# Two gated linear-attention blocks on one core: order of the last G addition, source of the gate weights, and a split transpose copy

## The chip, the cores and the metric

The kernel runs on one core of one Trainium2 chip. The metric is device time in microseconds (us), as the median of three runs. A profile is one further execution, recorded by the hardware profiler; its span is counted from its first to its last recorded instruction.

## The reference

Two linear-attention blocks A and B read the same input x (2048 rows, 640 columns, bf16) with weights of their own, and a gate per row mixes their outputs:

```python
x = A_x                                                  # (1, 2048, 640)
g = sigmoid((x * gate_w).sum(-1, keepdims=True))         # gate_w: 640 numbers
def block(x, wqkv, wo):                                  # H = 32 heads of 20
    q, k, v = heads(x @ wqkv)
    pq, pk = phi(q), phi(k)                              # phi(t) = (t + 1 if t > 0 else exp(t)) + 1e-6
    kv = einsum("bhsd,bhse->bhde", pk, v); z = pk.sum(over s)
    o = einsum("bhqd,bhde->bhqe", pq, kv) / (einsum("bhqd,bhd->bhq", pq, z) + 1e-6)
    return merge_heads(o) @ wo
return g * block(x, A_wqkv, A_wo) + (1 - g) * block(x, B_wqkv, B_wo)
```

## The kernel before

Rows are cut into 16 chunks of 128 (`ST = 16`) and columns into 5 (`DT = 5`). Matrix products run on TensorE in bf16 and gather in PSUM; ScalarE does exp and copies out of PSUM; VectorE does the rest of phi, sums and products; GpSimd builds masks at the start; SyncE issues nearly all transfers. The value projection is never formed: phi(k)^T v is worked out as (x^T phi(k))^T Wv, so each block needs G = x^T phi(k) (the tile `GT`, 640x640).

The stages, in order:

1. `k_first`: the first four chunks of x are loaded in plain form and transposed on TensorE (`x_transpose`, L187). Its copy out of PSUM (L194) is cut at the columns named in `cuts`; chunks 0 and 1 use two copies, chunks 2 and 3 one. The other 12 chunks of x^T come by 15 transposing transfers from SyncE (L129).
2. A's k projection by chunks (`k_chunk`, matmuls L209, phi L199, L202, L206), with parts of A's q (`q_block`, `q_unit`) between, up to chunk 14. Then SyncE loads the plain rows of x for the rest (L647), A's value and output weights and B's key weights.
3. From here the order of the instructions is the written one (`tc.manual_schedule`). `gate_columns` (L159) turns `gate_w` from a row into 32 equal columns per part, `gwr`: the row `grow` was loaded by GpSimd (L126) at the start, five matmuls of one partition multiply it by ones (L163), and VectorE casts the result out of PSUM (L166). Then comes chunk 15, the rest of A's q, with the gate's logits (`gate_pass`, matmuls L173) and the sums of phi(k) (`z_rows`).
4. `g_all`: A's G. Part of it is plain (`g_pass`), the rest a 2x2 scheme with seven products (`g_strassen`, matmuls L314, additions L331). Between the products, `norm_unit` spreads the reciprocals of the denominators over the rows (matmuls L487), ScalarE copies them to bf16 (L500), and VectorE multiplies them into phi(q) (L501). This is done five times, two copies and two products each.
5. B's k projection, with A's `kvt_pass` and `m_unit` between; B's q; B's G by the same code as A's.
6. The end: `kvt_pass` for B (matmuls L401, masks L409) starts as soon as all of B's `GT` is there; `m_unit` multiplies by `wo`; then 8 pairs of output chunks (class `Pair`, matmuls L512, additions L517), with sums of phi(q) and of the M tiles (`p_sums`, `m_sums`, all at L451) between.

The end of `g_strassen` differs between the blocks. For A, the last norm unit follows the last addition into `GT`. For B it precedes the last product:

```python
        if b == 1:
            norm()
        g_prod(even, SX[4], b22, False)
        add(GT[:, 0:2, hi], even, u2)
        if b == 0:
            norm()
```

PSUM is handed out as four slots in rotation (`turn`). The first sum after B's G is `p_sums(part[0], (1,))`, on VectorE.

Of the kernel before, what the change touches and what calls it, by code (L numbers as in the profile page):

```python
# [8 lines left out]
P = 128  # L9
FP32 = mybir.dt.float32  # L10
BF16 = mybir.dt.bfloat16
ACT = mybir.ActivationFunctionType
ALU = mybir.AluOpType

S, D, H = 2048, 640, 32
Dh = D // H
DT = D // P
ST = S // P
# [3 lines left out]
HF = D // 2  # L22
# [3 lines left out]
RB = 256  # L26
# [4 lines left out]
def kernel(  # L31
# [11 lines left out]
    nc = tc.nc  # L43
# [4 lines left out]
    persist = ctx.enter_context(tc.tile_pool(name="persist", bufs=1))  # L48
    wpool = ctx.enter_context(tc.tile_pool(name="wpool", bufs=1))
    work = ctx.enter_context(tc.tile_pool(name="work", bufs=2))  # L50
# [3 lines left out]
    turn = [0]  # L54

    def ps_raw(name, slot=None):

        if slot is None:
            slot = turn[0]
            turn[0] = (slot + 1) % 4  # L60
        return psum.tile([P, 4 * HB], BF16, tag=f"ps{slot}", name=name)

    def ps(name, slot=None):

        return ps_raw(name, slot).bitcast(FP32).rearrange("p (b n) -> p b n", b=2)
# [5 lines left out]
    GT = persist.tile([P, DT, D], BF16, name="GT")  # L71
# [7 lines left out]
    ones = persist.tile([P, H], BF16, name="ones")  # L79
    gwr = persist.tile([P, DT, H], BF16, name="gwr")  # L80
    D3 = persist.tile([P, DT, SH], BF16, name="D3")
    hc, ic = ST // 2, 2 * P
# [39 lines left out]
    load_x(nc.scalar, 3, 4)  # L122
    wq[0] = wpool.tile([P, DT, D], BF16, tag="wq", name="wqA")
    nc.sync.dma_start(out=wq[0][:], in_=wq_dram[0][:, :, 0:D])
    grow = work.tile([1, D], BF16, tag="zr", name="grow")
    nc.gpsimd.dma_start(out=grow[:], in_=gate_w.rearrange("(o f) -> o f", o=1))  # L126
    for n in range(1, NB):
        for c in range(DT):
            nc.sync.dma_start_transpose(  # L129
                out=xT[:, c, n * HB:(n + 1) * HB], in_=x2[n * HB:(n + 1) * HB, c * P:(c + 1) * P]  # L130
# [8 lines left out]
    for sign, base in ((1, 0), (-1, Dh - 1)):  # L139
        nc.gpsimd.affine_select(  # L140
            out=maskE[:], in_=maskE[:], pattern=[[sign * P, DT], [-sign * Dh, H]],
# [3 lines left out]
    for r in range(4):  # L145
        rows = slice(32 * r, 32 * r + 32)
        for sign, base in ((1, 0), (-1, Dh - 1)):
            nc.gpsimd.affine_select(
                out=E4[rows], in_=E4[rows], pattern=[[sign, D]],
# [5 lines left out]
    one_l, one_r = [nc.const_aps.tensor(1.0, [P, n], BF16) for n in (P, HB)]  # L155
    for k in range(7):
        nc.tensor.matmul(warm[:, 0, :], lhsT=one_l, rhs=one_r, start=True, stop=True)

    def gate_columns():  # L159

        gps = ps("gps")
        for c in range(DT):
            nc.tensor.matmul(  # L163
                gps[:, 0, c * H:(c + 1) * H], lhsT=grow[0:1, c * P:(c + 1) * P], rhs=ones[0:1, :], start=True, stop=True
            )
        nc.vector.tensor_copy(out=gwr[:], in_=gps[:, 0, 0:DT * H].rearrange("p (c h) -> p c h", h=H))  # L166

    def by_group(dst, lhsT, src, h):

# [17 lines left out]
    def x_transpose(i, slot, eng, cuts=(0, DT)):  # L187
        pt = ps_raw("xt", slot)
        for c in range(DT):
            nc.tensor.transpose(out=pt[:, c * P:(c + 1) * P], in_=xn[:, i, c * P:(c + 1) * P], identity=ident[:])  # L190
        copy = nc.scalar.copy if eng == "act" else nc.vector.tensor_copy
        src = pt[:, 0:D].rearrange("p (c n) -> p c n", c=DT)
        for lo, hi in zip(cuts, cuts[1:]):
            copy(out=xT[:, lo:hi, i * P:(i + 1) * P], in_=src[:, lo:hi])  # L194
# [13 lines left out]
    def k_mm(b, i, c, pt, hf):  # L208
        nc.tensor.matmul(  # L209
            pt[:, hf, 0:HF], lhsT=xT[:, c, i * P:(i + 1) * P], rhs=wk[b][:, c, hf * HF:(hf + 1) * HF],  # L210
            start=(c == 0), stop=(c == DT - 1),
        )

    def k_done(b, i, pt):
        phi(pk[:, i, :].rearrange("p (b n) -> p b n", b=2), pt[:, :, 0:HF], HF)

    def k_chunk(b, i, slot=None):
        pt = ps(f"k{'AB'[b]}", slot)
        for hf in range(2):
            for c in range(DT):  # L220
                k_mm(b, i, c, pt, hf)
        k_done(b, i, pt)

    def k_first():

        pts = [ps("kA", (2 + i) % 4) for i in (0, 1)]

        def part(i, cs):
            for c in cs:
                for hf in range(2):  # L230
                    k_mm(0, i, c, pts[i], hf)

        for i in range(2):
            x_transpose(i, i, "dve", (0, 2, DT))
        for i in range(2):
            part(i, (0, 1))
        x_transpose(2, 0, "dve")
        for i in range(2):
            part(i, (2,))
        pts.append(ps("kA", 1))  # L240
        part(2, (0, 1, 2))
        x_transpose(3, 0, "dve")
        for i in range(3):
            part(i, (3, 4))
            k_done(0, i, pts[i])
        k_chunk(0, 3, 0)
# [55 lines left out]
    def k_sum(b, k):  # L302

        b11, b12 = [pk[:, 0:hc, n * HF:(n + 1) * HF] for n in range(2)]
        b21, b22 = [pk[:, hc:ST, n * HF:(n + 1) * HF] for n in range(2)]
        t = TK[b]
        left, right = {1: lambda: (b12, b11), 2: lambda: (b22, t[1]), 3: lambda: (b22, b12), 4: lambda: (b21, t[2])}[k]()
        add_rows(t[k], left, right, ALU.subtract)

    def g_prod(pt, left, right, first):  # L310

        for i in range(hc):
            for n in range(2):
                nc.tensor.matmul(  # L314
                    pt[:, n, 0:HF], lhsT=left[:, i, n * P:(n + 1) * P], rhs=right[:, i, :],
                    start=(first and i == 0), stop=(i == hc - 1), skip_group_check=not first,
                )

    def g_strassen(b, norm):

        x11, x12 = [xn[:, k:k + hc, 0:ic] for k in (0, hc)]
        x22 = xn[:, hc:ST, ic:2 * ic]
        b11 = pk[:, 0:hc, 0:HF]
        b21, b22 = [pk[:, hc:ST, n * HF:(n + 1) * HF] for n in range(2)]
        lo, hi = slice(0, HF), slice(HF, D)

        def temp(name):
            return work.tile([P, 2, HF], FP32, tag="osb", name=name, bufs=3)

        def add(dst, pt, sb):  # L330
            nc.vector.tensor_tensor(out=dst, in0=pt[:, :, 0:HF], in1=sb[:], op=ALU.add)  # L331

        even, odd = ps("gs0", 0), ps("gs1", 1)
        g_prod(even, x11, b11, True)
        p1 = temp("p1")
        nc.scalar.copy(out=p1[:], in_=even[:, :, 0:HF])
        g_prod(odd, SX[2], TK[b][2], True)
        u2 = temp("u2")
        add(u2[:], odd, p1)
        k_sum(b, 4)  # L340
        norm()
        g_prod(even, x12, b21, False)
        nc.scalar.copy(out=GT[:, 0:2, lo], in_=even[:, :, 0:HF])
        norm()
        if b == 0:
            x_sum(4)
        g_prod(odd, SX[3], TK[b][3], False)
        u3 = temp("u3")
        add(u3[:], odd, p1)
        norm()  # L350
        even = ps("gs0", 0)
        g_prod(even, SX[1], TK[b][1], True)
        add(GT[:, 2:4, hi], even, u3)
        norm()
        g_prod(odd, x22, TK[b][4], False)
        add(GT[:, 2:4, lo], odd, p1)
        if b == 1:
            norm()
        g_prod(even, SX[4], b22, False)
        add(GT[:, 0:2, hi], even, u2)  # L360
        if b == 0:
            norm()

    def z_rows(b):

# [116 lines left out]
    def norm_unit(b, parts, rts, slots):  # L482

        pts = [ps(f"ex{'AB'[b]}", s) for s in slots]
        for k, (m, h) in enumerate(parts):
            for j in range(4):
                nc.tensor.matmul(  # L487
                    pts[j // 2][:, j % 2, k * RB:(k + 1) * RB], lhsT=E4[32 * j:32 * j + 32, m * P:(m + 1) * P],
                    rhs=rts[h][32 * j:32 * j + 32, :], start=True, stop=True,
                )  # L490
        (m0, h0), (m1, h1) = parts
        for jj in range(2):
            src = pts[jj][:].rearrange("p j (k n) -> p j k n", n=RB)
            if h0 == h1:
                r0 = h0 * 2 * HB + jj * HB
                dst = pqT[b][:, m0:m1 + 1, r0:r0 + HB].rearrange("p k (j n) -> p j k n", n=RB)
            else:
                dst = pqT[b][:, m0, :].rearrange("p (k u j n) -> p u j k n", k=2, u=2, n=RB)[:, jj]
            ex = work.tile([P, 2, 2, RB], BF16, tag="ex", name="ex")
            nc.scalar.copy(out=ex[:], in_=src)  # L500
            nc.vector.tensor_tensor(out=dst, in0=ex[:], in1=dst, op=ALU.mult)  # L501

    def rows_of(i):
# [131 lines left out]
    with tc.manual_schedule():  # L635
        k_first()
# [4 lines left out]
        for m in (0, 2):  # L641
            q_block(0, m, n)
    q_unit(0, DT - 1, 0)
    for i in range(hc, ST - 1):
        k_chunk(0, i)
    for n in range(1, NB):
        nc.sync.dma_start(  # L647
            out=xn[:, n * CB:(n + 1) * CB, :], in_=x2[n * HB:(n + 1) * HB, :].rearrange("(q p) d -> p q d", p=P)
        )
# [8 lines left out]
        return pool.tile([P, HB] if n == 1 else [P, n, HB], FP32, tag=name, name=name)  # L658

    with tc.manual_schedule():  # L660
        gate_columns()
        k_chunk(0, ST - 1)
        k_sum(0, 1)
        zsel = q_pass(0, [(m, 1) for m in range(DT)])
# [41 lines left out]
        with late_pool("single") as single:  # L706
            halves = [[bank(single, f"s{c}{hf}") for hf in range(2)] for c in (3, 4)]
            for c in (3, 4):
                pts = [t[:, 0:HF] for t in halves[c - 3]]
# [19 lines left out]
        for i in range(1, half):  # L729
            p, after = pairs[i], pairs[i + 1] if i + 1 < half else None  # L730
# [53 lines left out]
```

## Time and profile before

| what | before |
|---|---|
| median of 3 runs | 196.92 us (196.78 to 197.01) |
| profiled execution, its time | 196.04 us |
| its span | 194.3 us |
| granted TensorE clock, mean | 0.996 of full |
| TensorE busy | 97% of the span |
| VectorE busy | 80% |
| ScalarE busy | 44% |
| DMA queue 1 (SyncE) | 17694 packets, 13.34 MB, 25.2% of 16 engines' span |

A line of the timeline or of the chain begins with the start in us from the span's start and the duration in us. In the timeline follow engine (PE is TensorE, DVE VectorE, ACT ScalarE, POOL GpSimd, SPq SyncE's queue), line, operation, output and inputs with shapes, and the count, where neighbouring instructions are merged. A bracket gives how long the engine sat idle before, and what released it. Matmuls overlap, so their modelled ends may pass the start of the next. The chain of work that ended last is followed back from the last instruction; "issue" is time in which the engine waited for nothing that the profile shows.

### The profile page before, as it was taken

Reading aid. Unit: us, or ns where it says so; the run is one execution under the profiler, and the core shown is the slowest. Engines: PE = TensorE matmul, PEld = TensorE weight load, DVE = VectorE, ACT = ScalarE, POOL = GpSimd, SP = SyncE. Lnnn points to the kernel's source line nnn. Section 1 sums busy time; section 2 is a strip of 40 time slices with the busy share of each in tenths; the row PEclk is TensorE's granted clock in tenths of the full one; section 3 lists DMA queues with packets and bytes.
Section 4 is the critical chain, followed back from the end, with each engine's and each line's share of the span. In section 5 each row is a group of like instructions: output and inputs, shape, how many; then the busy total and the mean of one; then the engine's idle time right before and its main releaser. Section 6 shows DMA issues by size and latency. Waiting matters only on the chain.

```text
span 194.3 us, 3665 instructions
## 1 busy us (share of the span) xinstructions
PE 188.6 (97%) x1497; PEld 120.8 (62%) x1504; DVE 155.4 (80%) x258; ACT 84.9 (44%) x111; POOL 9.2 (5%) x23
## 2 busy tenths in 40 slices
PE   8999999999999999999999999999998999999992
PEld 3556557664576666877764444576667776777771
DVE  4388869888989796888786689999787899888553
ACT  2055455455931874356562455413874611111110
POOL 7920000000000000000000000000000000000000
PEclk9999999999999999999999999999999999999998
DMA  6975469960050000220062000000000001322112
GB/s 188 312 159 77 97 186 371 240 191 3 2 169 3 0 0 3 72 97 3 0 140 55 2 0 0 0 3 0 0 3 0 0 3 67 126 78 71 67 67 71
DMA packets 18318, 14.22 MB, mean 73 GB/s; under 512 B 8782, under 2 KB 18302, under 8 KB 18302
## 3 DMA queue, kind: packets, MB, share of 16 engines
q1 hardware_dynamic: 17694, 13.34, 25.2%
q10 hardware_dynamic: 576, 0.66, 1.0%
q8 instruction: 12, 0.20, 0.4%
q14 instruction: 4, 0.03, 0.1%
q0 software_dynamic: 32, 0.00, 0.0%
HBM read 9.40 MB, written 2.62 MB: 62 GB/s over the span
## 4 chain that ended last, share of the span: by engine, by line
PE 91%; DMA 2%; DVE 2%; issue 1%; ACT 1%; ACTq 0%; DVEq 0%
PE gs L314 15%; PE kB L209 11%; PE qB L254 11%; PE kA L209 11%; PE qA L254 7%; PE ox L512 5%; PE oy L512 5%; PE oz L512 5%; PE qA L265 4%; DMA xn<-in_A_x_dram 2%; PE ow L512 2%; PE gB L287 2%; PE gA L287 2%; PE mA L427 1%; DVE osb L517 1%; PE exB L487 1%
## 5 line engine op out<-in xcount | busy, mean ns | idle before, releaser
L209 PEld LDWEIGHTS <-xT 128*128 128x128 bf16 x320 | 30.8, 98 | 12.8 <-DVE xT L194 0.4
L202 DVE TENSOR_SCALAR e<-e 128x640 bf16<-128x640 bf16 (+1 forms) x52 | 18.8, 361 | 9.3 <-ACT e L199 8.3
L209 PE MATMUL kA<-wkA,xT 128*128 128x320 bf16 x160 | 23.0, 299 | 0.0
L209 PE MATMUL kB<-wkB,xT 128*128 128x320 bf16 x160 | 22.9, 299 | 0.0
L254 PE MATMUL qB<-xT,wqB 128*128 128x512 bf16 x97 | 21.9, 379 | 0.2
L199 ACT ACTIVATE e<-kA 128x640 bf16<-128x640 f32 x16 | 11.1, 704 | 13.6 <-PE kA L209 13.6
L254 PEld LDWEIGHTS <-wqB 128*128 128x128 bf16 x100 | 9.6, 98 | 11.4 <-issue 0.3
L199 ACT ACTIVATE e<-kB 128x640 bf16<-128x640 f32 x16 | 11.3, 705 | 10.7 <-PE kB L209 10.7
L199 ACT ACTIVATE e<-qB 128x1024 bf16<-128x1024 f32 x10 | 10.2, 1024 | 13.1 <-PE qB L254 10.7
L199 ACT ACTIVATE e<-qA 128x1024 bf16<-128x1024 f32 x10 | 10.2, 1024 | 10.5 <-PE qA L265 5.2
L206 DVE SCALAR_TENSOR_TENSOR pk<-kB,e 128x640 bf16<-128x640 f32 x16 | 13.2, 824 | 1.7
L206 DVE SCALAR_TENSOR_TENSOR pk<-kA,e 128x640 bf16<-128x640 f32 x16 | 13.2, 824 | 1.6
L254 PE MATMUL qA<-xT,wqA 128*128 128x512 bf16 x58 | 13.5, 379 | 0.1
L206 DVE SCALAR_TENSOR_TENSOR pqTB<-qB,e 128x1024 bf16<-128x1024 f32 x10 | 12.2, 1224 | 1.0
L549 ACT COPY u<-ox 128x320 f32<-128x320 f32 x8 | 3.4, 426 | 20.9 <-PE ox L512 20.9
L500 ACT CAST ex<-exA 128x1024 bf16<-128x1024 f32 x10 | 9.6, 1017 | 5.8 <-PE exA L487 4.9
L314 PEld LDWEIGHTS <-xn 128*128 128x128 bf16 x96 | 8.9, 98 | 4.5 <-issue 1.3
L314 PEld LDWEIGHTS <-S 128*128 128x128 bf16 x96 | 9.1, 98 | 4.2 <-issue 0.8
L500 ACT CAST ex<-exB 128x1024 bf16<-128x1024 f32 x10 | 9.6, 1017 | 3.7 <-PE exB L487 3.7
L512 PEld LDWEIGHTS <-xT 128*128 128x128 bf16 x85 | 8.0, 98 | 3.0 <-DVE xT L451 0.2
L254 PEld LDWEIGHTS <-wqA 128*128 128x128 bf16 x60 | 5.7, 97 | 6.7 <-issue 0.3
L512 PEld LDWEIGHTS <-pqTA 128*128 128x128 bf16 x85 | 8.0, 98 | 2.9
(118 smaller groups left out, 301.7 us busy)
## 6 DMA issues: line engine op xcount, KB each, us to landing
out_dram<-osb SPq DMA_DIRECT2D x15, 160.0 KB, 1.8
xn<-in_A_x_dram SPq DMA_DIRECT2D x3, 640.0 KB, 5.7
wqA<-in_A_wqkv_dram SPq DMA_DIRECT2D x1, 800.0 KB, 6.0
wvA<-in_A_wqkv_dram SPq DMA_DIRECT2D x1, 800.0 KB, 9.3
wkB<-in_B_wqkv_dram SPq DMA_DIRECT2D x1, 800.0 KB, 4.6
wqB<-in_B_wqkv_dram SPq DMA_DIRECT2D x1, 800.0 KB, 4.5
wvB<-in_B_wqkv_dram SPq DMA_DIRECT2D x1, 800.0 KB, 4.5
woA<-in_A_wo_dram SPq DMA_DIRECT2D x1, 750.0 KB, 12.0
```

Of the source, the lines that this page charges most:

```text
L199: nc.scalar.activation(out=e[:], in_=src, func=ACT.Exp)
L202: nc.vector.tensor_scalar(e[:], e[:], 1.0, EPS, op0=ALU.min, op1=ALU.add)
L206: nc.vector.scalar_tensor_tensor(out=dst, in0=src, scalar=1.0 + EPS, in1=e[:], op0=ALU.add, op1=ALU.max)
L209: nc.tensor.matmul(pt[:, hf, 0:HF], lhsT=xT[:, c, i * P:(i + 1) * P], rhs=wk[b][:, c, hf * HF:(hf + 1) * HF], start=(c == 0), stop=(c == D ...
L254: nc.tensor.matmul(pt[:, u, :], lhsT=wq[b][:, c, m * P:(m + 1) * P], rhs=xT[:, c, n * HB:(n + 1) * HB], start=(c == 0), stop=(c == DT - 1),)
L265: nc.tensor.matmul(pt[:, u, :], lhsT=wq[b][:, c, (m + u) * P:(m + u + 1) * P], rhs=xT[:, c, n * HB:(n + 1) * HB], start=(c == 0), stop=(c ...
L287: nc.tensor.matmul(pt[:, hf, 0:HF], lhsT=xn[:, i, c * P:(c + 1) * P], rhs=pk[:, i, hf * HF:(hf + 1) * HF], start=(i == 0), stop=(i == ST - 1),
L314: nc.tensor.matmul(pt[:, n, 0:HF], lhsT=left[:, i, n * P:(n + 1) * P], rhs=right[:, i, :], start=(first and i == 0), stop=(i == hc - 1), s ...
L427: nc.tensor.matmul(dst, lhsT=KVT[:rows, j, c * P:(c + 1) * P], rhs=wo_sb[b][:rows, j, hf * HF:(hf + 1) * HF], start=(k == 0), stop=(k == 1),)
L500: nc.scalar.copy(out=ex[:], in_=src)
L512: nc.tensor.matmul(dst, lhsT=left[:, c, r0:r0 + P], rhs=right[:, c, :], start=(first and c == 0), stop=(c == DT - 1), skip_group_check=not ...
L549: nc.scalar.copy(out=self.u2[:], in_=self.at("x"))
```

## The change

There are three edits.

- In `g_strassen`, the last addition into `GT[:, 0:2, hi]` becomes two, one per 128-row block. `norm_unit` no longer multiplies; it returns its two pending products, and a new function `scale` issues them. For every norm unit but B's last this leaves the order as it was. For B's last, the first product stays ahead of the last addition and the second goes behind it.
- `gate_columns`, its five matmuls and its cast are gone. `gate_w` is loaded as a tile `gcol` of 128 partitions by 5, one element at a time, by SyncE after the 15 transposes and before the plain rows of x. One VectorE copy spreads it over the 32 columns of `gwr`; it stands between the phi of chunk 14 and the phi of chunk 15. The slot that the gate's matmuls had is skipped.
- The copy of chunk 2's transposed x is cut in two, after 2 of 5 column parts, as for chunks 0 and 1.

```diff
-    grow = work.tile([1, D], BF16, tag="zr", name="grow")
-    nc.gpsimd.dma_start(out=grow[:], in_=gate_w.rearrange("(o f) -> o f", o=1))
+    gcol = persist.tile([P, DT], BF16, name="gcol")
...
-    def gate_columns():
-
-        gps = ps("gps")
-        for c in range(DT):
-            nc.tensor.matmul(
-                gps[:, 0, c * H:(c + 1) * H], lhsT=grow[0:1, c * P:(c + 1) * P], rhs=ones[0:1, :], start=True, stop=True
-            )
-        nc.vector.tensor_copy(out=gwr[:], in_=gps[:, 0, 0:DT * H].rearrange("p (c h) -> p c h", h=H))
...
-        x_transpose(2, 0, "dve")
+        x_transpose(2, 0, "dve", (0, 2, DT))
...
-        norm()
+        scale(norm())
...
         add(GT[:, 2:4, lo], odd, p1)
-        if b == 1:
-            norm()
+        late = norm() if b == 1 else []
+        scale(late[0:1])
         g_prod(even, SX[4], b22, False)
-        add(GT[:, 0:2, hi], even, u2)
-        if b == 0:
-            norm()
+        for n in range(2):
+            nc.vector.tensor_tensor(out=GT[:, n, hi], in0=even[:, n, 0:HF], in1=u2[:, n], op=ALU.add)
+        scale(late[1:] if b == 1 else norm())
...
+        muls = []
         for jj in range(2):
...
             ex = work.tile([P, 2, 2, RB], BF16, tag="ex", name="ex")
-            nc.scalar.copy(out=ex[:], in_=src)
+            nc.scalar.copy(out=ex[:], in_=pts[jj][:].rearrange("p j (k n) -> p j k n", n=RB))
+            muls.append((dst, ex))
+        return muls
+
+    def scale(muls):
+        for dst, ex in muls:
             nc.vector.tensor_tensor(out=dst, in0=ex[:], in1=dst, op=ALU.mult)
...
-    for i in range(hc, ST - 1):
+    for i in range(hc, ST - 2):
         k_chunk(0, i)
+    with nc.allow_non_contiguous_dma(reason="640 elements, one to a partition and column"):
+        nc.sync.dma_start(out=gcol[:], in_=gate_w.rearrange("(c p) -> p c", p=P))
...
     with tc.manual_schedule():
-        gate_columns()
+        k_chunk(0, ST - 2)
+        turn[0] = (turn[0] + 1) % 4
+        nc.vector.tensor_copy(out=gwr[:], in_=gcol[:, :, None].to_broadcast([P, DT, H]))
         k_chunk(0, ST - 1)
```

More of the change, by code (lines that the diff above doesn't have):

```diff
@@ L340, in g_strassen @@
         k_sum(b, 4)
-        norm()
+        scale(norm())
         g_prod(even, x12, b21, False)
         nc.scalar.copy(out=GT[:, 0:2, lo], in_=even[:, :, 0:HF])
-        norm()
+        scale(norm())
         if b == 0:
@@ L349, in g_strassen @@
         add(u3[:], odd, p1)
-        norm()
+        scale(norm())
         even = ps("gs0", 0)
@@ L353, in g_strassen @@
         add(GT[:, 2:4, hi], even, u3)
-        norm()
+        scale(norm())
         g_prod(odd, x22, TK[b][4], False)
         add(GT[:, 2:4, lo], odd, p1)
-        if b == 1:
-            norm()
+        late = norm() if b == 1 else []
+        scale(late[0:1])
         g_prod(even, SX[4], b22, False)
-        add(GT[:, 0:2, hi], even, u2)
-        if b == 0:
-            norm()
+        for n in range(2):
+            nc.vector.tensor_tensor(out=GT[:, n, hi], in0=even[:, n, 0:HF], in1=u2[:, n], op=ALU.add)
+        scale(late[1:] if b == 1 else norm())
     def z_rows(b):
@@ L491, in norm_unit @@
         (m0, h0), (m1, h1) = parts
+        muls = []
         for jj in range(2):
-            src = pts[jj][:].rearrange("p j (k n) -> p j k n", n=RB)
             if h0 == h1:
```

## The prediction

> **What bounds the kernel now.** I read the page first (busy shares, the chain by engine), then the chain in order of time to find the places where it leaves TensorE, then the timeline around each edit, and the SyncE queue last because one transfer is moved onto it. The built order of both kernels gave the order on each engine and which earlier instruction each one waits for.
>
> From the page, part 1 and the first line of part 4:
>
> ```profile
> PE 188.6 (97%) x1497; PEld 120.8 (62%) x1504; DVE 155.4 (80%) x258; ACT 84.9 (44%) x111; POOL 9.2 (5%) x23
> PE 91%; DMA 2%; DVE 2%; issue 1%; ACT 1%; ACTq 0%; DVEq 0%
> ```
>
> TensorE is busy 97% of the span and carries 91% of the chain. So an edit pays in two ways only: by taking matmuls away from TensorE, or by closing one of the few gaps in the chain. The chain in order of time (start, us, who) shows the three places that the diff touches:
>
> ```profile
> 7.04 0.54 PE kA L209 x4
> 7.58 0.04 issue
> 7.63 0.99 PE kA L209 x6
> ...
> 28.11 9.51 PE kA L209 x70
> 37.62 0.22 PE gps L163 x5
> 37.83 1.47 PE kA L209 x10
> 39.30 0.21 PE qA L254
> ...
> 147.49 0.69 DVE pqTB L501
> 148.18 0.74 DVE GT L331
> 148.92 0.04 issue
> 148.96 1.59 PE mid L401 x30
> ```
>
> The first is a tiny break, where chunk 2's transposed x is copied out. The second is the gate's five matmuls. The third is the one long stretch in the middle of the kernel in which the chain runs over VectorE: a normalisation product (L501), then the last addition of x^T phi(k) (L331), and only then B's kvt matmuls. The timeline there:
>
> ```profile
> 145.43 2.35 PE L314 MATMUL gs<-pk,MB 128*128 128x320 bf16 x16
> 147.49 0.69 DVE L501 TENSOR_TENSOR pqTB<-ex,pqTB 128x1024 bf16<-128x1024 bf16 x1 [0.22 <-ACT ex L500]
> 147.61 0.84 PE L512 MATMUL ox<-MA,pqTA 128*128 128x320 bf16 x5
> 148.10 0.81 DVE L331 TENSOR_TENSOR GT<-gs,u 128x640 bf16<-128x640 f32 x1
> 148.83 0.81 DVE L451 TENSOR_TENSOR pqTA<-pqTA,pqTB 128x1280 bf16<-128x1280 bf16 x1
> 148.96 1.59 PE L401 MATMUL mid<-GT,wvB 128*128 128x120 bf16 x30 [0.51 <-DVE GT L331]
> ```
>
> The addition's last input, the gs product, is ready at 145.43 + 2.35 = 147.78, but VectorE starts the addition at 148.10: a product that nothing waits for yet stands ahead of it. TensorE idles 0.51 us.
>
> **The change, part by part.**
>
> *B's last addition.* On TensorE and ScalarE the order is as before. On VectorE the last normalisation product goes behind the addition, and the addition becomes two of 128x320. By the built order the first waits for the last gs matmul of both blocks, the second for nothing more, and kvt's first matmul waits for the second. So there is no early start from the row blocks; the gain is the product moved out of the way. VectorE started a sum 0.04 us after its product's end at A's counterpart (75.33 after 70.84 + 4.45 = 75.29). So the first half starts at 147.82. Nearest row for its cost: osb<-oz, 128x320 out of PSUM, 490 ns, with the next one starting 0.41 later (159.07, 159.48). The second half runs from 148.23 to 148.72, and with the 0.05 that kvt took after the old addition (148.91 to 148.96) it starts at 148.77: **0.19 us** earlier. A single addition at 147.82 would end at 147.82 + 0.81 = 148.63, so the halving itself gives back 0.09. Bounds: the gain can't pass the idle 0.51; if the first half starts 0.10 late (as the u sum at 134.77 did behind two waits) and the halves do not overlap, kvt starts at 147.88 + 0.98 + 0.05 = 148.91 and the gain is 0.05. I take 0.19, since the pairs of L517 do overlap.
>
> What is queued behind: the product (starts 148.23 + 0.40 = 148.63; pairs of L501 lie 0.6 apart), then p_sums' addition at 149.23, which frees VectorE 0.73 later, at 149.96. The KVT masks need it when kvt's matmuls end, 148.77 + 1.59 = 150.36. That is 0.40 us of cover, where it was 0.95. Without it, the masks and then B's m_unit would come late by what is missing. ScalarE needs no buffer from the product before 157. In A the halved addition costs VectorE about 0.08 us at 75.33, and kvtA comes at 78.45: nothing.
>
> *The gate.* Five matmuls of one row each and their weight loads leave TensorE. From the end of chunk 14 to the first q matmul it took 39.30 - 37.62 = 1.68 us. A chunk without company takes 9.51 / 7 = 1.36. So **0.32 us** goes: the 0.22 of the matmuls and 0.10 of slower start of chunk 15. Low bound 0.22, high bound 0.40 (the weight loads' idle of 0.26 before them included in part). Chunk 15's PSUM slot is that of chunk 12, whose phi ended at 36.92, so it doesn't wait.
>
> VectorE's cast of gwr (314 ns) is replaced by a spread copy out of SBUF, moved one chunk later: behind chunk 14's phi, ahead of chunk 15's. The trace has no copy with a repeated input; I bound it by 0 and the 0.31 of the old cast, and take 0.31 (same 160 outputs). Chunk 14's phi frees VectorE at about 39.55, so gwr is there at about 39.9. The logit matmuls that read it start at 41.46 - 0.32 = 41.14: cover 1.2 us. Chunk 15's exp ends at 40.04 - 0.32 = 39.72, so its phi loses at most 0.15, and z's matmuls that read it come two us later: nothing.
>
> *The transfer* moves from GpSimd's queue to SyncE's, as 640 elements, between the transposes and x's rows:
>
> ```profile
> 4.34 20.95 SPq L129 DMA_TRANSPOSE xT<-in_A_x_dram  x15
> 25.33 1.68 SPq L647 DMA_DIRECT2D xn<-in_A_x_dram  x3
> 27.06 0.91 SPq L586 DMA_DIRECT2D wvA<-in_A_wqkv_dram  x1
> 28.01 0.97 SPq L591 DMA_DIRECT2D woA<-in_A_wo_dram  x1
> ```
>
> All transposes stay ahead of it. An issue costs 0.37 to 0.97 there. No row has a transfer of single elements. Bounds of its landing: 3.6 us (the old transfer of the same 1.2 KB) and 12.4 us (woA's last piece, the longest of all), so between 29 and 38 us, against 39.55 when VectorE wants it. Queue q1's packets took 25.2% of 16 x 194.3 us over 17694, or 44 ns each; 640 of them over 16 engines, spread evenly (an estimate), are 1.8 us, so I take the early end. It puts x's rows (5.7 us to landing) at some 33 to 36 us; their first reader is x_sum at 45.71. wvA, woA and wkB are wanted after 75. Nothing on the path. GpSimd loses a 0.61 us issue at 1.29; its identity was ready 1 us before the first transpose anyway.
>
> A rule speaks against this edit. The Trainium skill, "DMA: Bandwidth & Descriptors", section "Rules for kernel authors", says that a strided last dimension becomes one descriptor per element and should be made contiguous; its "Specifications" add that pieces under 512 B cost a read-modify-write. No run here shows such a transfer yet. By the rule it is slow, but only the second rival below would let that reach the time.
>
> *Chunk 2's copy in two* (292 and 348 ns in the rows of chunks 0 and 1, against 492): the first half is there at 7.08 + 0.29 = 7.37, before 7.58, and the second, wanted 4 matmuls later at 8.12, by about 7.7. The break of **0.04** closes. If the fourth chunk of x or wk's last piece lands just in time behind it, 0.
>
> Sum: 0.32 + 0.19 + 0.04 = **0.55 us**. The profiled execution took 196.04 with its span of 194.3 and would take 195.5; it lies 0.88 under the median of 196.92. The difference carries over, since later waits all hang on TensorE (ScalarE's exps wait for matmuls, VectorE for ScalarE): 196.4. About 0.2% (0.39 us) is what a measurement of this kernel can tell from no change.
>
> **The rivals.**
>
> 1. *It shrinks below what can be told.* Only the matmuls' own 0.22 goes (the 0.10 stays as a change-over elsewhere), the tail gives its low bound of 0.05, and the copy nothing: 0.27 us, 196.65. For it: the two steps of 0.10 rest on modelled ends. Against: chunks before it show 1.36 each without exception. Chance 0.23.
>
> 2. *Slower: the gate's column lands late.* VectorE then stands at the spread copy, with chunk 15's phi and k_sum behind it, and TensorE waits at the logits. It decides from a landing after 40.8 (41.14 less the copy): 15 us after issue at 25.4, or 360 ns per element on 16 engines, eight times the 44 ns. Were the elements served by only one engine, 640 x 44 ns = 28 us: landing near 54, 13 us late, 210 us. For it: no row of such a transfer. Against: even woA, queued behind five others, took 12.4. Chance 0.07.
>
> 3. *Row blocks do not pay:* the halves delay kvt and the product behind them pushes p_sums over the masks. VectorE would have to lose 0.40 more than counted; then kvt gains 0.19 and the masks lose it again: 0.36 in all, 196.56, within what can't be told. Chance 0.05.
>
> **How the numbers follow.** The forecast has 0.65 and gives "faster", its own range being a gain of 0.39 to 0.95 (0.40 + 0.51 + 0.04), 195.97 to 196.53. Rivals 1 and 3 are "same", 0.23 + 0.05. Rival 2, 0.07, is "slower"; nothing else here reaches that side. The range goes from 196.0, the high bounds, to 197.0, rival 1 with the spread of the runs above the median (0.09); it leaves out rival 2 and the edges.
>
> **What would show it.** In the changed profile: no gps; from the end of chunk 14 to the first q matmul 1.36 instead of 1.68; kvtB's mid 0.19 sooner after the last gs product, with VectorE's two 128x320 additions directly behind it and the last L501 product after them; masks waiting for mid and not for p_sums; no wait at 7.6; gcol landing before 38. A VectorE wait for a DMA near 39.5, masks behind p_sums, or a new TensorE gap at 43 or 57 would make it wrong.

## The result, and the profile after

| what | before | after |
|---|---|---|
| median of 10 runs each, on one chip | 196.89 us (196.18 to 197.44) | 195.69 us (194.78 to 196.60) |
| ratio | | 0.9936, interval 0.9913 to 0.9959 |
| profiled execution: time, span | 196.04, 194.3 us | 195.64, 193.8 us |

The change made the kernel faster by 1.26 us (0.81 to 1.71 by the interval). 0.55 was forecast, so the direction was right and the size was less than half of what came; 195.69 lies below the range. Two more timings of the same source gave 0.9937 each, and one of the kernel before 0.9993, so this is no accident of one run.

The page after, part 1, the first line of part 4, and two lines of part 3 (queue: packets, MB, share):

```profile
PE 189.2 (98%) x1499; PEld 121.2 (63%) x1499; DVE 155.6 (80%) x261; ACT 84.9 (44%) x111; POOL 8.5 (4%) x22
...
q1 hardware_dynamic: 18350, 13.34, 25.2%
...
q8 instruction: 11, 0.18, 0.4%
...
PE 96%; DVE 2%; ACT 0%; issue 0%; DVEq 0%; ACTq 0%
```

The step from 91% to 96% is no gain of that size. In this execution the chain runs back to the start over the warm-up matmuls, and in the one before over the landing of x's third chunk; which of the two comes last varies between executions of either kernel. Two smaller lines will matter below: q1 has 656 packets more (18350 for 17694), and q8 fetched 11 blocks of instructions where it was 12.

The chain of waits after, at the three places of the change:

```profile
7.08 0.28 PE xt L180 x5
7.36 1.38 PE kA L199 x10
...
9.01 2.99 PE kA L199 x22
...
28.22 10.87 PE kA L199 x80
39.09 2.16 PE qA L244 x10
...
145.29 2.29 PE gs L304 x16
147.59 0.02 issue
147.61 0.90 DVE GT L351 x2
148.51 0.04 issue
148.55 1.59 PE mid L391 x30
```

The ten matmuls behind chunk 2's transposes are one piece of 1.38; before they were 0.54, a break of 0.04, and 0.99. The weight loads of the last six of them, which need the copy, show what was closed (first before, then after; the bracket is the wait for the copy):

```profile
7.62 0.66 PEld L209 LDWEIGHTS <-xT 128*128 128x128 bf16 x6 [0.37 <-DVE xT L194]
```

```profile
7.74 0.66 PEld L199 LDWEIGHTS <-xT 128*128 128x128 bf16 x6 [0.17 <-DVE xT L184]
```

The gate's matmuls are gone from between chunks 14 and 15: 80 matmuls in 10.87, which is eight times 1.36. The last gs product is followed by the additions after 0.02 us, and there is no normalisation product in the chain any more. Note also that chunk 2's transposes start at 6.91 in the timeline here and at 6.59 in the profiled execution of before: this pair of spans (0.5 apart) hides some 0.3 us of the gain, since the execution after came to them later.

The timeline after B's last G product:

```profile
147.61 0.89 DVE L351 TENSOR_TENSOR GT<-gs,u 128x320 bf16<-128x320 f32 x2 [0.55 <-PE gs L304]
...
148.41 0.68 DVE L496 TENSOR_TENSOR pqTB<-ex,pqTB 128x1024 bf16<-128x1024 bf16 x1
148.55 1.59 PE L391 MATMUL mid<-GT,wvB 128*128 128x120 bf16 x30 [0.30 <-DVE GT L351]
...
150.18 0.66 DVE L399 TENSOR_TENSOR KVT<-mid,maskE 120x120 bf16<-120x120 f32 x3 [0.35 <-PE mid L391]
```

VectorE waits 0.55 for the product instead of being late for it, the product of phi(q) runs behind the additions, and the masks still wait for TensorE, with 0.35 us of cover left (0.40 was forecast).

SyncE's queue after, and VectorE's copy that replaces the cast:

```profile
4.36 21.02 SPq L128 DMA_TRANSPOSE xT<-in_A_x_dram  x15
25.42 0.58 SPq L642 DMA_DIRECT2D gcol<-in_gate_w_dram  x1
26.05 1.62 SPq L644 DMA_DIRECT2D xn<-in_A_x_dram  x3
```

```profile
39.68 0.31 DVE L660 COPY gwr<-gcol 128x160 bf16<-128x160 bf16 x1
```

The gate's column is issued at 25.42 in 0.58 us, lands 4.2 us after the start of its issue, and is read ten microseconds after that.

### The profile page after: what moved, and what is told of

The parts are those of the page before. It is cut to its first block, busy times and chain, and to the rows that moved or that the text cites. A ratio compares the mean times of both kernels' runs of the same rounds, so it can differ in the third digit from the quotient of the medians.

```text
span 193.8 us, 3662 instructions
## 1 busy us (share of the span) xinstructions
PE 189.2 (98%) x1499; PEld 121.2 (63%) x1499; DVE 155.6 (80%) x261; ACT 84.9 (44%) x111; POOL 8.5 (4%) x22
## 3 DMA queue, kind: packets, MB, share of 16 engines
q1 hardware_dynamic: 18350, 13.34, 25.2%
## 4 chain that ended last, share of the span: by engine, by line
PE 96%; DVE 2%; ACT 0%; issue 0%; DVEq 0%; ACTq 0%
PE gs L304 16%; PE kA L199 12%; PE kB L199 11%; PE qB L244 11%; PE qA L244 7%; PE ox L507 5%; PE oy L507 5%; PE oz L507 5%; PE qA L255 4%; PE ow L507 2%; PE gA L277 2%; PE gB L277 2%; PE warm L156 2%; PE mA L417 1%; DVE osb L512 1%; PE exA L477 1%
## 5 line engine op out<-in xcount | busy, mean ns | idle before, releaser
L199 PE MATMUL kA<-wkA,xT 128*128 128x320 bf16 x160 | 23.5, 307 | 0.0
L189 ACT ACTIVATE e<-qB 128x1024 bf16<-128x1024 f32 x10 | 10.2, 1024 | 13.1 <-PE qB L244 13.1
L189 ACT ACTIVATE e<-qA 128x1024 bf16<-128x1024 f32 x10 | 10.2, 1024 | 10.5 <-PE qA L255 5.2
## 6 DMA issues: line engine op xcount, KB each, us to landing
wvA<-in_A_wqkv_dram SPq DMA_DIRECT2D x1, 800.0 KB, 10.2
```

What stands on the lines that cost most here:

```text
L189: nc.scalar.activation(out=e[:], in_=src, func=ACT.Exp)
L199: nc.tensor.matmul(pt[:, hf, 0:HF], lhsT=xT[:, c, i * P:(i + 1) * P], rhs=wk[b][:, c, hf * HF:(hf + 1) * HF], start=(c == 0), stop=(c == D ...
```

## The experiments

After the result some 0.7 us (1.26 less 0.55) had no place. The runs below tell apart: terms that were mis-sized; a cost that GpSimd's early transfer had in the kernel before; a start that merely varies; and, at the end, an instruction fetch. All ratios are against the kernel before, run in turn on the same chip; 0.001 is 0.20 us.

| run | ratio | interval |
|---|---|---|
| e1 before, row loaded by SyncE late | 0.9996 | 0.9975 to 1.0017 |
| e2 after, with GpSimd's row load added | 0.9956 | 0.9935 to 0.9978 |
| e3 end of B's G alone | 0.9980 | 0.9961 to 0.9999 |
| e4 gate alone | 0.9972 | 0.9950 to 0.9993 |
| e5 cut copy alone | 0.9999 | 0.9980 to 1.0017 |
| e6, e10 after again | 0.9937, 0.9937 | 0.9912 to 0.9961, 0.9917 to 0.9956 |
| e7 before, ten warm-ups more | 1.0078 | 1.0053 to 1.0104 |
| e8 after, ten warm-ups more | 1.0037 | 1.0015 to 1.0058 |
| e9 before again | 0.9993 | 0.9969 to 1.0017 |
| e11 after, copy whole | 0.9957 | 0.9932 to 0.9983 |
| e12 after, addition whole | 0.9939 | 0.9916 to 0.9962 |
| e17 before, twenty TensorE instructions more | 0.9986 | 0.9967 to 1.0005 |
| e18 after, ten TensorE instructions more | 0.9961 | 0.9938 to 0.9984 |

**e1 and e2: the transfer on GpSimd.** The gate's five matmuls stay in e1, and only the row's load moves; e2 gives the kernel after an unused load of the row on GpSimd.

```diff
 e1, in before.py
-    nc.gpsimd.dma_start(out=grow[:], in_=gate_w.rearrange("(o f) -> o f", o=1))
+    ... the same by nc.sync, ahead of the plain rows of x
 e2, in after.py
+    grow = work.tile([1, D], BF16, tag="zr", name="grow")
+    nc.gpsimd.dma_start(out=grow[:], in_=gate_w.rearrange("(o f) -> o f", o=1))
```

> The kernel before with one edit: the row of gate weights is loaded by SyncE, after the transposes, and no longer by GpSimd at the start; the five matmuls stay. The change gave 1.2 us where its three steps add up to 0.55. Theory S: the other 0.65 is a cost of GpSimd's transfer at the start, which the profiled execution of before doesn't show; then this gives 0.65 us, a ratio of about 0.9967. Theory N: the steps give 0.55 and the rest is the spread of the executions; then this is 1.000. Theory T: the rest lies in the tail or at the gate's matmuls; then this is 1.000 too.

> The changed kernel with GpSimd's transfer of the row put back at the start; nothing reads the row. Theory S: only the three steps are left, 0.55 us, a ratio of about 0.9972, against 0.9936 for the change. Theories N and T: as the change itself, 0.9972 by N (its true size), 0.994 by T.

e1 does not move the time by anything that can be told, and its interval leaves out the 0.9967 of theory S: GpSimd's transfer does not cost 0.65 us, and that theory falls. The interval of e2 holds the forecasts of all three. Both traces come back below, where the end of the span shows a small cost that neither ratio resolves.

**e3, e4, e5: each part alone, and e6 after once more.**

```diff
 e3: before.py with g_strassen and norm_unit of after.py
 e4: before.py with gcol, its transfer and the gwr copy of after.py
 e5, in before.py
-        x_transpose(2, 0, "dve")
+        x_transpose(2, 0, "dve", (0, 2, DT))
```

> The kernel before with the edit at the end of the G scheme alone: last addition in two, ahead of the last normalisation product. Theories S and N: 0.19 us, a ratio of 0.9990; in the trace kvt for B starts about 3.33 us after the last gs product starts (3.53 before, 3.33 in the changed kernel). Theory T: up to 0.85 us, 0.9957.

> The kernel before with the edit of the gate alone: the weights as 128 by 5 elements by SyncE, no matmuls, one VectorE copy. Theory S: 0.32 + 0.65 = 0.97 us, 0.9951. Theory N: 0.32 us, 0.9984; in the trace 1.36 us from the end of chunk 14 to the first q matmul (1.68 before). Theory T with the rest at the matmuls: 0.97 us as well, but then the row by SyncE alone gives nothing.

> The kernel before with chunk 2's copy alone cut in two. The traces so far put ten matmuls of chunks 0 to 2 (from the transposes of chunk 2 to those of chunk 3) at 1.57 us with the whole copy and 1.37 us with the cut one. Theory P (the copy was worth 0.20 us and not 0.04): these ten take 1.37 us here, and the time falls by 0.20 us, a ratio of 0.9990. Theory of the prediction: 0.04 us, 0.9998. Theory D (what is left over, some 0.3 us, is that the cut copy also shortens the waits for the first loads): 0.5 us, 0.9975.

> The changed kernel once more, beside the kernel before. Theory P: 0.31 (gate) + 0.20 (end of G) + 0.20 (copy) = 0.71 us, a ratio of 0.9964. Theory D: about 1.0 us, 0.9949. The prediction's sum: 0.55 us, 0.9972.

By their ratios the gate alone gives 0.55 us (0.14 to 0.98), the end of G 0.39 (0.02 to 0.77), and the copy nothing that can be told. The stages in the traces are sharper than the times. From A's first q matmul to the logits every trace with the gate matmuls takes 29.57 us or more, and every one without them 29.25: 0.32. In e3 the additions start 0.02 after the product, as in after. From the start of the last sixteen gs matmuls to kvt it is 3.26 us in this chain as in that of after.

e5 looked like a copy that brings nothing. Its chain says otherwise:

```profile
7.47 1.38 PE kA L209 x10
...
10.44 0.80 DVE e L202
...
12.23 4.48 PE qA L265 x20
```

The ten matmuls did shrink to 1.38. But chunk 0's `e` sum on VectorE, 0.33 us in the profile of before, took 0.80 here, so that chunk 0's phi, and with it the PSUM slot of the q product, came late and took 0.27 us back (0.11 ahead of the q product, which is 12.23 less 9.13 and the usual 2.99, and 0.16 within it). This happens without the cut copy too: the sum took 0.58 in e9, 0.67 in e17 and 0.77 in e15. It cost the path 0.07 to 0.27 in 4 of the 10 traces of kernels that keep the gate matmuls (e5, e9, e15, e17), 0.07 on average over all ten, and nothing in the 10 without them (e4's took 0.50, and it was hidden). Over the ten traces with GpSimd's load, which have e2 in place of e1, the average is the same.

The traces also show what held it. GpSimd is at its mask selects then, about 0.71 us each, as here in e15:

```profile
9.56 0.71 POOL L148 TENSOR_SCALAR_AFFINE_SELECT E<-E 32x640 bf16<-32x640 bf16 x1
9.69 0.77 DVE L202 TENSOR_SCALAR e<-e 128x640 bf16<-128x640 bf16 x1 [0.79 <-ACT e L199]
```

In the eight traces in which the sum took over 0.33 (e4, e5, e6, e9, e13, e14, e15, e17: 0.35 to 0.79), it began inside a select and ended 0.18 us after the end of that same select. Where it began outside a select, or within the last 0.11 us of one (before, e2, e3, e16), it took 0.33; in before, e2 and e3 the next select was longer in its turn, 0.78 to 0.83, and ended 0.58 after the sum. So the sum and a select hold each other up. The transfer of the row decides where they meet: with GpSimd's load its last two selects run from 9.55 to 11.17 at the widest, without it from 8.44 to 9.97, and with the usual start the sum begins between 9.6 and 10.6.

**e11 and e12: after, with one part taken back.**

```diff
 e11, in after.py
-        x_transpose(2, 0, "dve", (0, 2, DT))
+        x_transpose(2, 0, "dve")
 e12, in after.py
-        for n in range(2):
-            nc.vector.tensor_tensor(out=GT[:, n, hi], in0=even[:, n, 0:HF], in1=u2[:, n], op=ALU.add)
+        add(GT[:, 0:2, hi], even, u2)
```

> The changed kernel with chunk 2's copy whole again, so gate and end of G together. Theory P: 0.51 us against the kernel before, 0.9974; in the trace the ten matmuls between the transposes of chunks 2 and 3 take 1.57 us. Theory R with the remainder tied to the cut copy (it pays more once GpSimd's masks end at 9.9 and not at 11.1 us, because chunk 0's phi then finds VectorE free): 0.51 us here and 1.05 with it. Theory R with the remainder elsewhere: 0.8 us, 0.9958.

> The changed kernel with the last addition of G whole again, still ahead of the last normalisation product. The prediction priced the halving at 0.09 us; the changed kernel's trace has the two halves at 0.90 us (147.61 to 148.51) against 0.75 for a whole addition ahead of kvt in the kernel before. So kvt for B should start 0.08 to 0.15 us sooner after the last gs product (3.33 us after its start in the changed kernel), and the time be that much less than the changed kernel's: 0.9942 to 0.996, hardly to be told from it by the times alone.

With the copy whole the chain has its old form again, at the same place in the same kernel:

```profile
7.15 0.54 PE kA L199 x4
7.69 0.04 issue
7.74 0.99 PE kA L199 x6
```

1.57 us against 1.38 (1.37 in e12): 0.20 by the timeline, not the 0.04 of the break. The time went up by 0.4 us with an interval that holds 0.2. The whole addition costs VectorE 0.82, and kvt starts 3.19 after the gs piece instead of 3.26:

```profile
147.28 0.82 DVE L321 TENSOR_TENSOR GT<-gs,u 128x640 bf16<-128x640 f32 x1 [0.55 <-PE gs L304]
148.03 0.68 DVE L495 TENSOR_TENSOR pqTB<-ex,pqTB 128x1024 bf16<-128x1024 bf16 x1
```

So the halving gives back 0.06 to 0.07 (0.09 was forecast), and all of that part's gain is the product moved out of the way. In the time, 0.9939 against 0.9937, it can't be told; e12 is the version I would keep, but it is not shown to be faster.

**e7, e8: a late start; e9, e10: controls; e13 to e16: single executions.** In e7 and e8 TensorE warms up with 17 matmuls instead of 7, so that x's chunks are there whenever they land. e9 and e13 to e15 are the kernel before, e10 and e16 the kernel after. The single executions took 195.83, 196.59 and 195.90 us before and 194.98 after.

```diff
 e7 in before.py, e8 in after.py
-    for k in range(7):
+    for k in range(17):
```

> The kernel before with 17 warm-up matmuls on constants in place of 7, so that TensorE turns to the first rows of x at about 8.2 us, when their loads have landed. The time should rise by about 2 us. If the spread of the executions (0.4 us standard deviation) comes from the landing of the first loads, it falls to 0.2 us or less; if not, it stays.

> The changed kernel with 17 warm-up matmuls. Against the kernel before with 17 of them: theory P 0.71 us less (or 0.51, if the cut copy has nothing left to close), theory D the same 0.5 to 0.7 us, because no load is waited for; a gain near 1.0 us here too would put the remainder into the steps themselves.

> The kernel before, run as if it were an experiment: a second look at its first 10 us and its end, and a measure of what the comparison calls a difference where there is none. All theories: 1.000, within 0.002.

> The changed kernel a third time, for its true size. Theory P (sum of what the traces show: 0.31 gate, 0.20 end of G, 0.20 copy): 0.71 us, 0.9964. Theory R (some 0.3 us more than the sum, not yet placed): 1.05 us, 0.9946.

> A further profiled execution of the kernel before, to see where its executions differ from one another. Theory P: from the start of the 22 matmuls of chunks 0 to 3 to the last matmul it takes 179.1 us as always, and what differs is when these 22 start (8.3 to 9.1 us so far) and the 6.2 to 6.5 us after the last matmul. Theory R (the remainder of 0.4 us sits in the body of the kernel in some executions): the body takes longer than 179.2 us in some of these looks, with a new wait of TensorE to name.

> As the look before it: body 179.1 us by theory P, more in some by theory R.

> As the look before it: body 179.1 us by theory P, more in some by theory R.

> A further profiled execution of the changed kernel: body 178.57 us, start of the 22 matmuls between 8.4 and 9.1 us, 6.2 us after the last matmul.

The spread did not fall with the late start (0.5 to 0.6 us of standard deviation in both), so waiting for x is not all that makes it. The time of e7 rose by 1.5 us where about 2 was forecast. The difference of e7 and e8 is 0.0041, or 0.81 us. Neither trace has a held sum, or a fetch near its last outputs (told below), so of the terms of the table below those left are the gate, the end of G, the copy and GpSimd's queue: 0.86.

The start itself varies: chunk 2's transposes begin at 6.00 to 7.02 us in the timelines of all traces but these two. In 11 of these 18 they wait for the landing of x's third chunk, in 7 for the matmuls ahead. These run late where the clock steps up late: the trace's record of the granted clock steps to full between 3.6 and 6.8 us after the span's start, and up to that step (6.8 us in after) the kA matmuls start 0.27 us apart, behind it 0.14. So the first eight take 1.26 to 1.37 us in most traces and 1.59 to 2.17 in five (after, e1, e2, e13, e14), of both kernels. The Trainium skill, "TensorE: Matmul & The Clock Gate", section "Part 1: The HAM clock gate", says that the clock steps up at the end of a free-running window of about 3.4 us, so at a varying time; the traces agree, with steps spread over 3.2 us.

The single executions were taken to compare the rest stage by stage. Behind the three places of the change it is the same in all traces to 0.02 us (from B's first kvt matmul to the queue step ahead of ScalarE's last copy of u, 39.03 to 39.04), except at the very end. SyncE issues the last output chunk in two halves of 320 columns, and the first of these issues is not the same in all. The line of SyncE's timeline for it (start, duration) in before, and in e14, which is the same kernel:

```profile
190.97 0.44 SPq L576 DMA_DIRECT2D out_dram<-osb  x1
```

```profile
190.77 1.07 SPq L576 DMA_DIRECT2D out_dram<-osb  x1
```

and in after:

```profile
190.56 0.42 SPq L571 DMA_DIRECT2D out_dram<-osb  x1
```

This issue is 0.42 in all nine traces of kernels without the gate matmuls up to e16. In the eight with them and the old start (before, e1, e3, e5, e9, e13, e14, e15) it is 0.44, 0.71, 0.42, 0.65, 0.53, 0.47, 1.07 and 0.55: 0.605 on average, 0.18 more. No edit is there. What is there is one packet of q8, as the DMA view of e14 between 189.5 and 191.5 us has it:

```profile
q1 hardware_dynamic: 73, 0.09, 13.4%
q8 instruction: 1, 0.02, 2.9%
```

2.9% of 16 engines over 2 us is 0.93 us on one engine. It starts at 190.53, 0.23 us ahead of the 1.07 issue. In before it starts 0.82 ahead (190.14), and in the other six 0.75 to 0.99 ahead. In after there is none. The traces of e2 and e12, which also lack the gate matmuls, have the twelfth packet 1.2 and 1.7 us after the end of the span. In e7, with twenty TensorE instructions more, it is 2.58 ahead, and the issue takes 0.42.

**e17, e18: the fetch put elsewhere.** The warm-up keeps its length in columns and changes only its number of instructions (each matmul is two: weights and product).

```diff
 e17, in before.py
-    for k in range(7):
-        nc.tensor.matmul(warm[:, 0, :], lhsT=one_l, rhs=one_r, start=True, stop=True)
+    for k in range(17):
+        nc.tensor.matmul(warm[:, 0, :211], lhsT=one_l, rhs=one_r[:, :211], start=True, stop=True)
 e18, in after.py: the same with range(12) and 299 columns
```

> The kernel before with 17 warm-up matmuls of 211 columns instead of 7 of 512 (3587 columns for 3584, twenty TensorE instructions more). Theory F (fetch): in the kernel before, a 16 KB instruction fetch of queue q8 starts 0.2 to 1.0 us ahead of SyncE's issue of the last 320-column output and lengthens that issue (0.42 to 1.07 us); the ten TensorE instructions that the gate change drops put that fetch past the end. Twenty instructions more move it ahead instead, as in the late start of before, where it began 2.59 us ahead: the issue takes 0.42, and the end, from the start of ScalarE's last copy of u, 6.2 to 6.35 us instead of 6.31 to 6.91; the time about 0.15 under the kernel before, ratio 0.999. Rival V (the length of the end is spread, or comes from the gate column): the issue takes 0.44 to 1.07 as in most traces with the gate matmuls, the end 6.3 to 6.9, ratio 1.000.

> The kernel after with 12 warm-up matmuls of 299 columns instead of 7 of 512 (3588 columns for 3584, ten TensorE instructions more, so as many as the kernel before has). Theory F: a q8 fetch starts again within about 1 us ahead of the issue of the last 320-column output (twelve fetches instead of eleven), that issue takes 0.42 to 1.07 us with a mean near 0.58 instead of 0.42 in all nine traces without the gate matmuls, and the end takes 6.3 to 6.9 instead of 6.13 to 6.28; the time 0.15 to 0.25 over the kernel after, ratio 0.995 against before. Rival V: eleven fetches or twelve, the issue stays at 0.42 and the end at 6.13 to 6.28, ratio 0.994.

e17, the kernel before with more to do, has its fetch 1.88 us ahead, and its issue is that of after:

```profile
191.49 0.42 SPq L576 DMA_DIRECT2D out_dram<-osb  x1
```

e18, the kernel after with as many TensorE instructions as before, has its twelfth fetch back, 1.06 us ahead of the issue, and the issue is longer than in any other trace without the gate matmuls:

```profile
190.41 0.49 SPq L571 DMA_DIRECT2D out_dram<-osb  x1
```

The issues of both traces moved as the fetch theory said, and both ratios too (0.28 us faster, 0.47 us slower than e6), though a ratio alone can tell neither from nothing. The ends, counted as in the expectations from the queue step ahead of ScalarE's last copy of u, are 6.31 in e17 and 6.23 in e18. The first lies in the windows of both theories. The latter lies in the rival's window and 0.07 short of the fetch theory's; that window was taken from kernels that all have the second cost of the end, told next, which e18 lacks, and 6.23 is the 6.18 of after with 0.06 for the longer issue.

One execution of each is thin, but the end of the packet settles it. In the eight traces in which the packet still runs when this issue begins (before, e1, e5, e9, e13, e14, e15, e18), the issue ends 0.30 to 0.39 us after the packet's end; in the four in which it has ended (e3, e7, e8, e17), the issue takes 0.42. The fetch ahead of that one, near 172 us, does the same to an earlier output's issue in nine traces of both kernels, which ends 0.37 to 0.40 after the packet; there nothing waits for it. In e6 the packet runs from 172.20 to 173.16, and the issue, 0.33 elsewhere, takes 0.92:

```profile
172.62 0.92 SPq L576 DMA_DIRECT2D out_dram<-osb  x1
```

The issue directly ahead of each of these, which starts 0.4 to 0.7 us sooner and meets the packet too, keeps its 0.33.

The rest of the end was in these traces all along. From the end of SyncE's last issue to the end of the span it is 2.40 to 2.42 us in the nine traces of kernels that load the row by GpSimd and keep the gate matmuls, and 2.26 to 2.28 in the nine without that load other than e1. e1, which is before without that load and nothing else, has 2.27, and e2, which is after with it, 2.34. So one small transfer on GpSimd's queue at the start costs 0.14 us after the last output in the kernel before, and 0.06 in the kernel after. The traces show part of what is done in that time: GpSimd's closing instruction, which clears a range of semaphores, takes 0.14 us in all ten traces with the load and 0.10 in all ten without, and SyncE has one more wait of 0.06 behind the last landing in those nine.

## Why the prediction was right or wrong

| term | forecast | by the traces |
|---|---|---|
| gate matmuls | 0.32 | 0.32 |
| end of B's G | 0.19 | 0.21 |
| cut copy of chunk 2 | 0.04 | 0.20 |
| fetch off the last issue | not seen | 0.18 on average |
| GpSimd's queue at the end | not seen | 0.13 |
| chunk 0's sum not held up | not seen | 0.07 on average |
| sum | 0.55 | 1.11 |

1.11 lies inside the measured 0.81 to 1.71. As a test of the sum: five profiled executions of before (with e9, e13, e14, e15) have a mean span of 194.29 and four of after (with e6, e10, e16) of 193.51, 0.78 apart; chunk 2's transposes began 0.34 later in the latter four (6.66 against 6.32), and 0.78 + 0.34 = 1.12. That shows that no stage is left out, not that each term has exactly its size.

- *The step that failed first is the copy's term.* The text read the 0.04 of the break and took that as all there was. But the break is counted from the modelled end of the matmul ahead, 0.30 us after its start, while matmuls that wait for nothing start 0.14 apart. From start to start the fourth and fifth matmul lie 0.34 apart before (7.28, 7.63) and 0.14 after (7.60, 7.74), and the wait of the weight load fell from 0.37 to 0.17: 0.20 either way. The six matmuls behind the wait keep the usual pace in both. The lines quoted in the prediction already had it: 0.54, 0.04 and 0.99 add up to 1.57, where ten matmuls at the rate of a chunk take 1.36. The range was wrong with it: the bounds on the copy were 0 and 0.04.
- *The second, and the larger with 0.38 us, is the list of what leaves with an edit.* Five matmuls and a transfer were priced on their own engine at their own time; of the transfer the prediction says that GpSimd "loses a 0.61 us issue", and puts that at nothing. The matmuls also take ten instructions out of TensorE's stream, which moved a fetch past the end: 0.18. The transfer was the only one of GpSimd's queue, which costs 0.13 at the end, and it had pushed GpSimd's mask selects onto chunk 0's sum: 0.07. The page of before had the twelve blocks of q8 in it, but not what they meant. The Trainium skill, "Runtime: NRT & Kernel Launch", section "Instruction fetch mechanics", says that each engine's stream is fetched in 16 KiB blocks of 256 instructions by a queue of its own, mostly hidden. The 0.02 MB per packet agree, and TensorE itself shows no cost of it here (39.03 to 39.04 us for the stage above, wherever the fetches fall); what is not hidden is what the block does to another engine's issue.
- *The gate* went as worked out, the 0.10 of the slower chunk 15 included: the doubt behind rival 1, that only 0.22 would go, did not come true.
- *The end of B's G* went as worked out: additions 0.04 after the product in the timeline, two halves in 0.89 (0.90 forecast), kvt 0.21 sooner after the start of the last gs product (3.33 for 3.54 in the traces' rows; the chain counts from a little later), cover of the masks 0.35 (0.40 forecast). Rival 3 did not happen.
- *The transfer* landed near the early bound, 4.2 us after issue. The rule weighed in the prediction holds as far as it goes: the queue has 656 packets more, and behind it x's rows took 6.6 us to land instead of 5.7 and wvA 10.2 instead of 9.3. Over all traces the difference is 0.6 to 0.7 on average, with ranges that overlap. Nothing on the path waited for them, so rival 2 did not happen. (Its 360 ns per element should be about 380: 15.4 us over 40 elements on each engine.)
- *The carry-over.* "Later waits all hang on TensorE" was right for the two parts it was said of. But the profiled execution, 0.88 under the median, was taken as a fair sample of the stalls. That one shows less than the kernel has on average: the issue of the last output took 0.44 there and 0.605 on average, and chunk 0's sum was undisturbed. Which of the two a profiled execution meets is chance; this one met next to nothing of either.

What stays open: why an issue waits for the fetch's packet, and the one directly ahead of it does not; and whether the later mean start in the traces with the cut copy (6.73 over eight, 6.47 over ten without) is more than chance. If it were not chance, the copy's 0.20 would be spent again there, and e5's ratio does not exclude that. With the late start the order is the other way (8.16 in e7, 7.96 in e8 with the cut copy).

## What to carry to other kernels

A break in the chain of matmuls is counted from a modelled end and shows less than the stall: add up the pieces on both sides of it, and compare them with the same work elsewhere. When an edit takes instructions or the only transfer of a queue away, look also at what else that engine does beside others, and at the ends of the program, at what the fetches and queues do there, and expect some tenths of a microsecond either way. And take the stalls to be priced from several executions: one profile shows those that happened to it.

## What the runs showed of the hardware

- One 16 KB instruction fetch took 0.88 to 1.52 us on one DMA engine. An output transfer that SyncE began to issue while it ran, 0.4 to 0.7 us behind another, ended its issue 0.30 to 0.40 us after the fetch's packet (17 cases in 20 traces), so that it took up to 1.07 us to issue, against 0.33 or 0.42 elsewhere. Twenty instructions more made the kernel before no slower (e17).
- One transfer of 1.2 KB on GpSimd's queue at the start makes the span end about 0.14 us later in the kernel before (2.41 against 2.27 from the last issue) and 0.06 in the kernel after (2.34 against 2.28).
- A transfer of 640 single elements from SyncE took 0.58 us to issue and 3.1 to 5.1 us to land (4.2 in after), and the transfers behind it took 0.6 to 0.7 us longer to land on average.
- A 128x640 sum of bf16 on VectorE that takes 0.33 us took up to 0.79 when it began while GpSimd was at a mask select, and then ended 0.18 us after that select (eight traces); a select that followed such a sum closely took 0.78 to 0.83 instead of 0.71 (three traces).
- Up to the step of the granted clock to full, at 3.6 to 6.8 us, matmuls of 320 columns start 0.27 us apart, behind it 0.14.
